# One mask product per attention unit instead of two, and wider sums of h, in a fused attention and SwiGLU kernel

## The chip, the cores and the metric

The kernel runs on one core of a Trainium2 chip. The metric is device time in microseconds (us) of one execution. Four runs of the kernel before are at hand, with their median, and one further execution was taken with the hardware profiler.

## What is computed

The reference is sliding-window attention with a linear distance bias, followed by a SwiGLU feed-forward block. All inputs and the output are float32; the kernel works in float16 with float32 accumulation.

```python
# q, k, v: (8, 8, 576, 64)
scores = (1.0 / np.sqrt(D)) * np.matmul(q, k.transpose(0, 1, 3, 2))
rel = pos[:, None] - pos[None, :]
bias = slopes[:, None, None] * (-np.abs(rel))[None]
mask = (rel >= 0) & (rel < 128)
scores = np.where(mask, scores + bias[None], -1000000000.0)
attn = softmax(scores)                         # max, exp, division by the sum
x = np.matmul(attn, v)                         # then to (4608 tokens, 512)
# w_gate, w_val: (512, 1536), w_out: (1536, 512)
g = x @ w_gate
out = (g * sigmoid(g) * (x @ w_val)) @ w_out
```

## The kernel before

**Attention.** The work is cut into 36 units `i = 9*s + p`: four pairs of sequences `s`, and nine key tiles `p` of 128 rows in each. `scores(i)` writes the score products of all eight heads, 256 queries to a key tile, into four PSUM banks of the pool `ps_a` (tag `a`, four banks in all). ScalarE then takes four exponentials, `act(0,0)`, `act(0,1)`, `act(1,0)`, `act(1,1)` (L284), one for each bank, into the tile `ex` of 128 x 2048 float16 values (eight heads of 256). The mask and the bias are multiplied in afterwards, in place, as exp(bias) from the table `m_reg` (L290, on VectorE): `mul(0)` takes the first four heads after the second exponential, `mul(1)` the other four after the fourth. Units `p` = 3, 7 and 8 have 128 queries and one product at L321 instead, and the units below 4 add the bias in the matmul. `weighted(i)` multiplies with v (PE, L345), VectorE takes the reciprocal of the sums (L347) and scales (L348) into `x`. From unit `LATE` = 13 on, `weighted(i)` is issued in the middle of the scores of unit i+1. `x` is transposed into `xT` on PE (L371) with a copy on ScalarE (L375), or by DMA from SyncE's queue (L366) from unit 24 on.

**Feed-forward.** The tokens form nine blocks `n` of 512. In blocks 0 to 5, for each of the twelve tiles `m` of 128 hidden columns, PE writes `pg` and `pv` (L397; pool `ps_f`, tag `gv`, three banks), ScalarE takes a tanh (L415), VectorE makes `uu` (L416) and `hT` (L427), which free the banks. Block 0 is projected plainly (L451). For blocks 1 to 8 the output product is made by a seven-product scheme (`strassen`, L532). It needs sums of the four quarters of `hT`: per group of tiles four VectorE instructions, L485 to L488, where L486 adds in place into `hT` and L487 and L488 use what L486 and L487 have written. `strassen(n, t)` is spread over the steps of block n+1. Its two accumulators X and Y share one PSUM bank (tile `po`, one buffer), so a product into Y waits until VectorE has read X, and the next product into X until VectorE has read Y. VectorE's additions from X and Y at L536 carry the names `p5s` and `u2s`. Blocks 6 to 8 make gate and value by seven products too (L623), with sums of the weights (L597 to L600) that are made beforehand in block 5 and its neighbours.

**Sums before.** `sums(n, c)` covers two tiles of the lower and two of the upper half of the twelve; it is issued in blocks 1 to 5 at m = 9, 10 and 11 with c = 0, 1, 2, so that each L485 to L488 there handles 128 x 512 values. Except at m = 9 and 10 of block 1, where they are issued at once, the instructions go into the list `later` and leave it one or two at a time at each half step. They come before the third product of the `strassen` of that block. Blocks 6 to 8 issue their sums in another place, in the same groups of two tiles.

**Order.** Generators interleave attention and feed-forward steps. The order on PE is written out from step 60 on, which is near the start of block 2; VectorE, ScalarE and SyncE are ordered by a list scheduler on its own cost estimates at build time, and each engine then runs its queue strictly in that order. VectorE's queue as built is thus fixed before the run: an instruction whose input is not ready holds up all that stand behind it.

Of the kernel before, what the change touches and what calls it, by code (L numbers as in the profile page):

```python
# [36 lines left out]
LATE = 13  # L37
# [14 lines left out]
def kernel(  # L52
# [190 lines left out]
    def scores(i):  # L243

        s, p = units[i]
        def combined(n):
            return scores_128(s, (3, 7, 8)[n], 8, (s, "c", n), msk[n])

        def together(one, two):
            return [one[0] + two[0]] + one[1:] + two[1:]  # L250

        if p == 8:
            first = combined(0) if s == 0 else []
            return first + together(combined(1), combined(2))
        if p == 7 and s == 0:
            return scores_128(s, p, p, (s, p), reg[:, :, 0:P])
        if p == 7:
            return together(scores_128(s, p, p, (s, p), reg[:, :, 0:P]), combined(0))
        if p == 3:
            return scores_128(s, p, p, (s, p), reg[:, :, 0:P], i < FIRST)  # L260
        ks = (9 * s + p) % NK
        banks = []
        early_tile = i < FIRST
        e = epool.tile([P, H, 256], FP16, name="ex", tag="ex", bufs=4)
        ex[(s, p)] = e

        def products():
            for q4 in range(2):
                two = [ps_a.tile([P, 2, 256], FP32, name="ps", tag="a") for _ in range(2)]
                banks.append(two)  # L270
                for par in range(2 if early_tile else 0):
                    o = 4 * q4 + 2 * par
                    nc.tensor.matmul(two[par], idm, bias[:, o:o + 2, :], start=True, stop=False)
                for j in range(2):
                    pair = 2 * q4 + j
                    for par in range(2):
                        rows = slice(64 * par, 64 * par + 64)
                        nc.tensor.matmul(two[par][:, j, :], kT[rows, ks, pair, :],  # L278
                                         qT[rows, p:p + 2, pair, :], start=(j == 0 and not early_tile),
                                         stop=(j == 1))  # L280

        def act(q4, par):
            o = 4 * q4 + 2 * par
            nc.scalar.activation(e[:, o:o + 2, :], banks[q4][par], AF.Exp, scale=scale)  # L284

        def mul(q4):
            if early_tile:
                return
            o = slice(4 * q4, 4 * q4 + 4)
            nc.vector.tensor_mul(e[:, o, :], e[:, o, :], reg[:, o, :])  # L290

        return [[products], [lambda: act(0, 0)], [lambda: act(0, 1), lambda: mul(0)],
                [lambda: act(1, 0)], [lambda: act(1, 1), lambda: mul(1)]]

    def scores_128(s, kt, qt, key, m, early_tile=False):

        ks = (9 * s + kt) % NK
        banks = []
        e = epool.tile([P, H, P], FP16, name="exc", tag="exc", bufs=5)
        ex[key] = e  # L300

        er4 = e.rearrange("k (a par b) q -> k a par b q", a=2, par=2)

        def products():
            banks.extend(ps_a.tile([P, 4, P], FP32, name="psc", tag="a") for _ in range(2))
            for par in range(2 if early_tile else 0):
                nc.tensor.matmul(banks[par].rearrange("k (a b) q -> k a b q", a=2), idm,
                                 bias.rearrange("k (a par b) q -> k a par b q", a=2, par=2)
                                 [:, :, par, :, 0:P], start=True, stop=False)
            for j in range(4):  # L310
                for par in range(2):
                    rows = slice(64 * par, 64 * par + 64)
                    nc.tensor.matmul(banks[par][:, j, :], kT[rows, ks, j, :], qT[rows, qt, j, :],  # L313
                                     start=(j == 0 and not early_tile), stop=(j == 3))

        def act(par):
            nc.scalar.activation(er4[:, :, par], banks[par].rearrange("k (a b) q -> k a b q", a=2),  # L317
                                 AF.Exp, scale=scale)

        return [[products], [lambda: act(0)],  # L320
                [lambda: act(1), lambda: early_tile or nc.vector.tensor_mul(e, e, m)]]  # L321
# [140 lines left out]
    HM = NMB // 2  # L462
# [28 lines left out]
        for f in fs:  # L491
            f()

    def sums(n, c):

        if n not in hsum:
            hsum[n] = [spool.tile([P, HM, 256], FP16, name=f"S{i}", tag=f"S{i}") for i in (2, 3, 4)]
        lo, hi = slice(2 * c, 2 * c + 2), slice(HM + 2 * c, HM + 2 * c + 2)
        a11, a12 = hT[n][:, lo, 0:256], hT[n][:, hi, 0:256]
        a21, a22 = hT[n][:, lo, 256:512], hT[n][:, hi, 256:512]  # L500
        s2, s3, s4 = (t_[:, lo, :] for t_ in hsum[n])
        return four_sums(a11, a12, a21, a22, s2, s3, s4)
# [106 lines left out]
    later = []  # L609
# [91 lines left out]
    def ffn():  # L701

        for n in range(NBLK):
            if n > 1:
                parts = chain(strassen(n - 1, 0), strassen(n - 1, 1))
            if n == 1:
                for j in range(PRE):
                    for _ in project(0, j, ps_f, "po", 1):
                        yield 1.0
            if n == SEVEN_FROM:  # L710
                break
            for m in range(NMB):
                for half, _ in enumerate(gate_val(n, m)):
                    yield 1.0
                    if n > 1 and 2 * m + half in AT:
                        next(parts)
                        yield 0.75
                    if n > 1:
                        for _ in range(1 + (len(later) > 3)):
                            if later:  # L720
                                later.pop(0)()
                if n == 1:
                    if m in (4, 6, 8, 10):
                        for _ in project(0, m // 2 - 2, ps_f, "po", 1):
                            yield 1.0
                    if m in (4, 6, 8):
                        weight_sums(m // 2 - 2)
                if n > 0 and m >= 9:
                    (at_once if n == 1 and m < 11 else later.extend)(sums(n, m - 9))
                if n + 1 == SEVEN_FROM:  # L730
                    if m == SILU_AT:
                        attention_ends()
                        by_silu.update((n, i) for i in range(m + 1, NMB))
                    if m in (SILU_AT + 1, SILU_AT + 2):
                        later.extend(gate_val_weight_sums(m - SILU_AT - 1))
                    if m == SILU_AT:
                        later.extend(x_sums(n + 1))
            if n > 1:
                assert next(parts, 0) == 0
        ends = [strassen(NBLK - 1, t) for t in range(2)]  # L740
        final = ()
        for n, k, name, which in seven_steps():
            if k == 0 and n > SEVEN_FROM:
                assert next(parts, 0) == 0
                parts = chain(strassen(n - 1, 0), strassen(n - 1, 1))
            if n == SEVEN_FROM and k in (1, 3, 10, 17):
                later.extend(gate_val_weight_sums(2 + (k + 4) // 7))
            yield 0.5
            if k % 3 == 2 and k < 42:
                next(parts)  # L750
                yield 0.75
            if k == 20 and n + 1 < NBLK:
                later.extend(x_sums(n + 1))
            if k == 35:
                later.extend(sums(n, 0))
            if name == "fourth" and which is not None and which[1] > 3:
                if which == (NBLK - 1, 5):
                    at_once(final)
                else:
                    later.extend(sums(which[0], which[1] - 3))  # L760
            if n == NBLK - 1 and k == 40:
                final = sums(n, 2)
                later.append(final.pop(0))
            for _ in range(2 if len(later) > 4 or k >= 39 or k < 7 else 1):
                if later:
                    later.pop(0)()
            if n == NBLK - 1 and k == 41:
                next(ends[0])
                yield 0.75
        assert next(parts, 0) == 0 and not later  # L770

        for t in (1, 0, 1, 0, 0, 0, 1, 0, 0, 1, 1, 1, 1):
            next(ends[t])
            yield 0.75
# [230 lines left out]
```

## Time and profile before

| what | value |
|---|---|
| median of 4 runs | 345.08 us (344.95 to 345.47) |
| profiled execution, device time | 344.82 us |
| span of the profile, first to last instruction | 343.0 us |
| granted TensorE clock | 1.000 |
| PE busy | 329.7 us, 2983 matmuls |
| VectorE (DVE) busy | 277.3 us, 652 instructions |
| ScalarE (ACT) busy | 207.7 us, 412 instructions |
| mask products L290, 128 x 1024 | 42, mean 685 ns |
| sums L485 to L488 of hT, 128 x 512 | 24 on each line, mean 415 ns |

The device time is 1.82 us more than the span. By the first `pg` product of each, block 1 runs from 56.5 to 95.5 us, block 2 to 134.4, block 3 to 172.9, block 4 to 210.1 and block 5 to 245; what follows, to 343 us, is blocks 6 to 8. A row of the list of instructions in time gives the start, the time from the first start to the last end of the merged instructions, the engine, the line, what is written and read, the count, and in brackets the idle time of the engine before it with what ended it. [...]

### The profile page before, as it was taken

The page shows a single profiled execution, that of the slowest core. Times are in us where ns is not written, and L with a number is a line of the kernel's source. Part 1 is how long each engine was busy: PE and PEld are TensorE (multiplying, and loading weights), DVE is VectorE, ACT ScalarE, POOL GpSimd, SP SyncE. Part 2 cuts the span into 40 slices and gives each one's busy share as a digit, 9 for nine tenths or more (in the row PEclk, how much of TensorE's full clock was granted, in tenths as well). Part 3 has the DMA queues.
Part 4 walks back from the last instruction along what each step waited for, and adds up shares of the span by engine and source line. Part 5 has one row for each costly group of instructions (what it writes and reads, how often), then busy time and mean ns, then how long its engine had stood idle before and what let it go on. Part 6 is the DMA issues. An engine that isn't in the chain of part 4 may idle for free.

```text
span 343.0 us, 7778 instructions
## 1 busy us (share of the span) xinstructions
PE 329.7 (96%) x2983; PEld 218.7 (64%) x2983; DVE 277.3 (81%) x652; ACT 207.7 (61%) x412; POOL 109.8 (32%) x136
## 2 busy tenths in 40 slices
PE   7999989999999999999999999999999999999995
PEld 4484445444456565656565655565788878888884
DVE  5578886999798679988899999999855975775683
ACT  3758676565666765756556547563467666776640
POOL 8968672639775176743017000000000000000000
PEclk9999999999999999999999999999999999999999
DMA  9999999999999999999949914021101101011014
GB/s 152 169 180 175 161 173 149 83 131 149 153 174 152 158 179 164 162 167 148 185 111 104 176 32 78 15 69 41 63 2 61 63 0 64 7 57 63 0 70 116
DMA packets 160037, 37.37 MB, mean 109 GB/s; under 512 B 147328, under 2 KB 155648, under 8 KB 160000
## 3 DMA queue, kind: packets, MB, share of 16 engines
q0 software_dynamic: 118336, 18.62, 82.5%
q1 hardware_dynamic: 40976, 17.64, 28.6%
q10 hardware_dynamic: 688, 0.62, 0.6%
q8 instruction: 23, 0.38, 0.5%
q14 instruction: 14, 0.11, 0.1%
HBM read 37.91 MB, written 9.44 MB: 138 GB/s over the span
## 4 chain that ended last, share of the span: by engine, by line
PE 70%; DVE 19%; ACT 6%; issue 3%; DMA 1%; ACTq 0%; DVEq 0%
PE po L532 15%; PE pg L397 13%; PE pv L397 12%; PE gX L623 8%; PE gY L623 4%; PE av L345 4%; DVE uu L416 3%; DVE hT L427 3%; PE ps L278 3%; PE p L532 2%; PE po L451 2%; PE gZ L623 2%; DVE x L348 2%; ACT ex L284 2%; PE px L371 2%
## 5 line engine op out<-in xcount | busy, mean ns | idle before, releaser
L397 PE MATMUL pv<-xT,wv_sb 128*128 128x512 f16 (+2 forms) x320 | 76.5, 358 | 0.6 <-DVE uu L416 0.2
L397 PE MATMUL pg<-xT,wg_sb 128*128 128x512 f16 (+2 forms) x320 | 75.8, 358 | 0.3 <-DVE xT L373 0.2
L415 ACT ACTIVATE tt<-pg 128x512 f16<-128x512 f32 (+2 forms) x70 | 41.3, 590 | 50.4 <-PE pg L397 49.5
L284 ACT ACTIVATE ex<-ps 128x512 f16<-128x512 f32 x96 | 50.0, 604 | 11.4 <-PE ps L278 11.4
L416 DVE SCALAR_TENSOR_TENSOR uu<-tt,pg 128x512 f16<-128x512 f16 (+2 forms) x69 | 45.8, 664 | 10.5 <-ACT tt L415 10.2
L427 DVE TENSOR_TENSOR hT<-uu,pv 128x512 f16<-128x512 f16 (+2 forms) x70 | 46.5, 665 | 3.6 <-PE pv L397 1.6
L185 POOL DMA_DIRECT2D va<-in_v_dram x40 | 34.3, 862 | 39.1 <-PE av L345 30.5
L397 PEld LDWEIGHTS <-wg_sb 128*128 128x128 f16 x320 | 28.2, 98 | 24.4 <-issue 2.6
L397 PEld LDWEIGHTS <-wv_sb 128*128 128x128 f16 x320 | 28.3, 98 | 24.1 <-issue 2.9
L532 PEld LDWEIGHTS <-hT 128*128 128x128 f16 x384 | 36.8, 98 | 10.4 <-issue 1.1
L191 POOL DMA_DIRECT2D kn<-in_k_dram x39 | 33.3, 858 | 19.1 <-DMA kT<-kn 11.6
L191 POOL DMA_DIRECT2D qn<-in_q_dram x39 | 33.4, 863 | 15.2 <-DMA va<-in_v_dram 7.8
L532 PEld LDWEIGHTS <-S 128*128 128x128 f16 x288 | 27.7, 98 | 10.6 <-issue 2.5
L290 DVE TENSOR_TENSOR ex<-ex,m_reg 128x1024 f16<-128x1024 f16 x42 | 28.6, 685 | 3.2 <-ACT ex L284 3.1
L348 DVE TENSOR_TENSOR x<-av,rec 128x256 f16<-128x256 f32 x72 | 28.5, 418 | 0.4
L532 PE MATMUL po<-T,S 128*128 128x256 f16 x192 | 26.5, 273 | 0.5 <-DVE S L487 0.5
L532 PE MATMUL po<-T,hT 128*128 128x256 f16 x192 | 26.1, 273 | 0.0
L317 ACT ACTIVATE exc<-psc 128x512 f16<-128x512 f32 x40 | 21.3, 606 | 4.1 <-PE psc L313 4.1
L675 DVE TENSOR_TENSOR hT<-s,v 128x512 f16<-128x512 f16 x18 | 7.6, 422 | 18.5 <-ACT s L674 18.5
L345 PEld LDWEIGHTS <-ex 128*128 128x128 f16 x384 | 17.4, 97 | 4.6 <-issue 1.3
L345 PE MATMUL av<-va,ex 128*128 128x65 f16 x384 | 19.3, 193 | 0.7 <-ACT ex L284 0.7
L278 PE MATMUL ps<-qT,kT 64*128 64x256 f16 x192 | 16.5, 272 | 0.4 <-DVE qT L223 0.2
(134 smaller groups left out, 535.8 us busy)
## 6 DMA issues: line engine op xcount, KB each, us to landing
out_dram<-osb SPq DMA_DIRECT2D x32, 256.0 KB, 2.6
va<-in_v_dram POOLq DMA_DIRECT2D x32, 128.0 KB, 7.9
qn<-in_q_dram POOLq DMA_DIRECT2D x31, 128.0 KB, 8.1
kn<-in_k_dram POOLq DMA_DIRECT2D x31, 128.0 KB, 8.2
wg_sb<-in_moe_w_gate_dram POOLq DMA_DIRECT2D x6, 256.0 KB, 7.6
wv_sb<-in_moe_w_val_dram POOLq DMA_DIRECT2D x6, 256.0 KB, 8.2
wo_sb<-in_moe_w_out_dram POOLq DMA_DIRECT2D x2, 768.0 KB, 9.2
kn<-in_k_dram POOLq DMA_DIRECT2D x8, 64.0 KB, 7.6
```

The costliest lines, as they stand in the source:

```text
L185: nc.gpsimd.dma_start(va[rank][p0:p1, :, 0:D], src)
L191: nc.gpsimd.dma_start(t_[p0:p1], src)
L284: nc.scalar.activation(e[:, o:o + 2, :], banks[q4][par], AF.Exp, scale=scale)
L290: nc.vector.tensor_mul(e[:, o, :], e[:, o, :], reg[:, o, :])
L345: nc.tensor.matmul(av[:, j, :], w, val, start=(n == 0), stop=(n == len(todo) - 1))
L348: nc.vector.tensor_mul(x[:, 4 * half:4 * half + 4, :], av[:, :, 0:D], rec.broadcast_to([P, 4, D]))
L397: nc.tensor.matmul(ps[:, c0:c1], w[:, kb, ms], xT[n][:, kb, c0:c1], start=(kb == 0 and c0 == 0), stop=(kb == NKB - 1 and c1 == 512), skip_ ...
L415: nc.scalar.activation(tt, pg[:, c0:c1], AF.Tanh, scale=0.5)
L416: nc.vector.scalar_tensor_tensor(out=uu, in0=tt, scalar=one if (n, m) == PIN else 1.0, in1=pg[:, c0:c1], op0=ALU.add, op1=ALU.mult)
L427: nc.vector.tensor_mul(hT[n][:, m, c0:c1], acted[(n, m)][1][:, c0:c1], pv[:, c0:c1])
L532: nc.tensor.matmul(dst, a[:, m, cols], b[:, m, :], start=(start and m == 0), stop=(m == HM - 1), skip_group_check=True)
L623: nc.tensor.matmul(dst[:, i, :], w[:, kb, c0 + i * P:c0 + (i + 1) * P], a[:, kb, :], start=(start and i == 0 and kb == 0), stop=(i == 1 an ...
```

## The change

From unit 13 on, `mul(0)` does nothing and `mul(1)`, after the fourth exponential, multiplies all eight heads in one instruction of 128 x 2048 values. This concerns 15 of the 21 units that have L290 products. In blocks 1 to 5 the sums are issued at m = 10 for four tiles of each half (128 x 1024 values in each instruction) and at m = 11 for the remaining two, instead of three times two tiles at m = 9, 10 and 11. The arithmetic on each value is the same.

```diff
@@ scores(i) @@
         def mul(q4):
-            if early_tile:
+            if early_tile or (q4 == 0 and i >= LATE):
                 return
-            o = slice(4 * q4, 4 * q4 + 4)
+            o = slice(0, 8) if i >= LATE else slice(4 * q4, 4 * q4 + 4)
             nc.vector.tensor_mul(e[:, o, :], e[:, o, :], reg[:, o, :])
@@ sums @@
-    def sums(n, c):
+    def sums(n, c, many=2):
...
-        lo, hi = slice(2 * c, 2 * c + 2), slice(HM + 2 * c, HM + 2 * c + 2)
+        lo, hi = slice(2 * c, 2 * c + many), slice(HM + 2 * c, HM + 2 * c + many)
@@ ffn() @@
-                if n > 0 and m >= 9:
-                    (at_once if n == 1 and m < 11 else later.extend)(sums(n, m - 9))
+                if n > 0 and m >= 10:
+                    (at_once if n == 1 and m < 11 else later.extend)(sums(n, 2 * m - 20, 24 - 2 * m))
```

## The prediction

> **What bounds the kernel now.** I read the page's busy shares first, then who PE waits for, then the instructions in time around each wait.
>
> ```profile
> span 343.0 us, 7778 instructions
> PE 329.7 (96%) x2983; PEld 218.7 (64%) x2983; DVE 277.3 (81%) x652; ACT 207.7 (61%) x412; POOL 109.8 (32%) x136
> PEclk9999999999999999999999999999999999999999
> ```
>
> PE is the bound: busy 96% at the full granted clock, and four 512-wide products follow each other in 0.86 us all through the chain. VectorE (DVE) has the second load. The windows tell where the two meet:
>
> ```profile
> 100.00:130.00 30.00, 29.28 (x288) 18.52 (x286) 23.35 (x53) 19.18 (x39) 15.14 (x20) 1.00 1.93 162
> 165.00:194.00 29.00, 27.54 (x247) 16.73 (x245) 28.86 (x73) 15.72 (x33) 7.61 (x10) 1.00 1.50 135
> ```
>
> The columns are PE, weight loads, DVE, ACT, POOL. From 100 to 130 us DVE is busy 23.35 of 30 us; from 165 to 194 it is full. A saving on DVE can only take away waits of PE, and in the part that the change touches (84 to 243 us) these are all that the profile lists (us in total, times, longest):
>
> ```profile
> PE po L532 <- DVE osb L536: 1.5, 2, 0.8
> PE p L532 <- ACT ex L284: 0.7, 1, 0.7
> PE av L345 <- ACT ex L284: 0.7, 2, 0.5
> PE po L532 <- DVE S L487: 0.5, 1, 0.5
> PE px L371 <- DVE x L348: 0.2, 1, 0.2
> PE psc L313 <- DVE osb L536: 0.2, 1, 0.2
> ```
>
> So 2.4 us of waits belong to DVE and 1.4 us to ACT. More than 2.4 us cannot come from a lighter DVE.
>
> **What one instruction less is worth.** The starts of DVE's neighbours in block 1:
>
> ```profile
> 81.03 0.68 DVE L290 TENSOR_TENSOR ex<-ex,m_reg 128x1024 f16<-128x1024 f16 x1
> 81.63 0.41 DVE L486 TENSOR_TENSOR hT<-hT 128x512 f16<-128x512 f16 x1
> 81.97 0.42 DVE L485 TENSOR_TENSOR S<-hT 128x512 f16<-128x512 f16 x1
> 82.31 0.42 DVE L487 TENSOR_TENSOR S<-hT 128x512 f16<-128x512 f16 x1
> ```
>
> The next start is 0.605 us after the 1024-wide product and 0.336 us after a 512-wide sum (81.63 to 82.31 is two of them). So 512 values more cost 0.269 us, and the part paid once per instruction is 0.067 us. The means of 685 and 415 ns would make it 0.145, but they overlap the next start by 0.08 us, so the starts count. A 2048-wide product, which the trace does not show, then takes 0.605 + 2 x 0.269 = 1.14 us of DVE; bounds are 1.08 (twice the slope of values alone, nothing per instruction) and 1.37 (twice the mean of 685). I take the line through the starts, since it is the same operation on the same tiles. The change removes 15 products and 5 x 4 = 20 sums: 35 x 0.067 = 2.3 us of DVE, 5.1 by the means. In a stretch where DVE idles this is worth nothing.
>
> [...]
>
> **What the merged product costs.** It starts only after the fourth exponential, where the first half started after the second, and nothing behind it can pass. I followed the changed kernel's instruction order, as it is built, through all 15 places. The place that counts is in block 2, DVE first, then ACT, then PE:
>
> ```profile
> 126.50 0.69 DVE L416 SCALAR_TENSOR_TENSOR uu<-tt,pg 128x512 f16<-128x512 f16 x1 [1.68 <-ACT tt L415]
> 127.47 0.69 DVE L290 TENSOR_TENSOR ex<-ex,m_reg 128x1024 f16<-128x1024 f16 x1 [0.29 <-ACT ex L284]
> 128.09 0.68 DVE L427 TENSOR_TENSOR hT<-uu,pv 128x512 f16<-128x512 f16 x1
> 128.68 0.42 DVE L536 SCALAR_TENSOR_TENSOR osb<-po,p5s 128x256 f32<-128x256 f32 x1
> ```
> ```profile
> 126.36 2.06 ACT L284 ACTIVATE ex<-ps 128x512 f16<-128x512 f32 x4
> ```
> ```profile
> 128.10 1.02 PE L397 MATMUL pg<-xT,wg_sb 128*128 128x512 f16 x4
> 129.15 0.81 PE L532 MATMUL po<-wo_sb,S 128*128 128x256 f16 x6
> ```
>
> Before, the `p5s` addition ends at 129.10, and PE, free at 129.12, starts its product into the shared bank at 129.15. DVE had just idled 1.68 us there. After, the order is uu, hT, the whole product, then `p5s` (the second half stood behind it before). hT starts at 127.37, as its product ends at 127.34. The whole product starts when the exponentials end, 126.36 + 2.06 = 128.42, plus 0.03; the addition starts 1.14 us later, at 129.59, and ends at 130.01. PE's product starts at 130.05: **+0.90 us**, between 0.84 and 1.13 by the bounds of the product. Queued behind on DVE are reciprocals, x and uu, which PE needs 2 us later; on PE everything is behind.
>
> Elsewhere the cover holds or nearly. The product delays what follows it by up to 0.53 us where its first half used to run during the third and fourth exponential. Behind it `p5s` at 148.82 has 0.53 us until PE needs it (**+0.05** for the edge), x at 181.09 is 0.24 us early and moves by 0.29 (**+0.05**), `p5s` at 205.09 has 0.38 and moves by 0.30, `uu`, `hT` and x elsewhere have 0.4 us and more. If a cover is gone, each costs what it lacks, at most 0.3 us.
>
> **Block 1.** Here the scheduler also reorders PE between 87.4 and 93 us. On DVE x at 85.25 comes 0.33 us earlier, and px with it, but the next product waits for an exponential that ends at 86.27, as before: 0. Then in the new order four of the po products, not five, stand ahead of the av products, and the second pair of ps waits for its bank until 88.77 (first exponential from 88.17). That gives the first av at 89.36 for 89.79, and the second at 89.82 for 90.04, as its exponential ends at 89.76. From there PE runs seven po (1.51), eight pg and pv (1.72), px and av (0.45) without a wait, to the ps at 93.50 for 93.86. The x copy on ACT now stands behind the tanh, ends at 93.80 and frees the bank of the last four ps. The exponentials start at 93.91 for 94.28, and av follows at 94.56 for 94.93: **-0.37 us**. It is between 0 (the queue slips back behind one of these waits) and -0.6 (all the ACT wait of 0.46, and one change of product kind, 0.1). The whole product there ends 0.2 us before PE needs the x behind it; if not, +0.3 at most.
>
> **Where DVE is full.** From 130 to 143 us the removed instructions and the later PE put DVE 0.57 us ahead, which ends PE's wait for x at 142.9: ps starts there at 143.01 and 143.33, 0.10 and 0.19 late, of which I take **-0.25**. From 164.7 to 188.2 DVE never idles; six instructions less (four sums, two products) give 0.40 us, but the new order pulls one more weight sum (L599, 0.34, right behind the one that it needs) ahead of `p5s`, so the wait of 0.84 us at 187.8 stays: 0. From 205 to 217.5 the sums and products give 0.40, but the product at 201.6 now starts with the fourth exponential (201.97) and ends 0.31 later: **-0.06** on the 0.5 us wait for S at 217.4. The wait of 0.62 at 167.2 begins with an ACT wait, not with load: 0. Transposes and stores on SyncE's queue keep their count; in block 1 three transposes move ahead of a store, whose data come later anyway. POOL's order is the same. The ACT wait of 0.7 at 118 stands behind a tanh, not behind DVE, and after 243 nothing is changed: 0.
>
> **The sum.** -0.37 + 0.90 + 0.05 + 0.05 - 0.25 - 0.06 = +0.32 us on the profiled 344.82 (343.0 span and 1.82 around it), so 345.1. The median of the runs is 345.08, 0.26 above that execution, and on it I predict **345.4 us**. With the ends of the terms the case spans -0.5 to +1.6: 344.6 to 346.7. A measurement of this kernel tells about 0.2%, 0.7 us, from no change, so most of the case lies within that.
>
> [...]
>
> **Rivals.** *Relief reaches PE.* In the full stretches the 0.40 us saved shows at 187.8 and again at 217.4, with -0.37 and -0.25 of above, and the whole product does not stand in PE's way: -1.4, so 343.7. For it speaks that 1.5 us of the waits lie there; against it the order as built, with the product ahead of `p5s` and L599 pulled forward. 18%. *The merged product holds PE up at more places.* If it takes 1.23 us and not 1.14 (twice the mean of 685 less one time the 0.145 that the means give per instruction), the wait in block 2 is 0.99 and the thin covers give way: 0.14 at 149, 0.14 at 181, 0.01 at 205; with block 1 at 0 and the -0.25 kept that is +1.0: 346.1. It decides from some 0.1 us of extra length on; against it speaks that the starts of the 512- and 1024-wide rows leave no room for it. 30%. *The change does not do what it says*, in that the scheduler splits or duplicates work: excluded, as the built order has 15 products of 2048 and 617 DVE instructions for 652. The forecast has 52%.
>
> **Numbers.** 0.2% of the median puts the bounds at 344.4 and 345.8. The first rival's 343.7 lies below, the second's 346.1 above, and a sixth of the forecast's own case (-0.5 to +1.6, likeliest +0.3) lies above too. Faster by over 0.2%: 0.18; within: 0.46; slower: 0.36. The range 344.0 to 346.5 leaves out some half of the first rival and the ends of the others.
>
> **What would show it.** Right: L290 at 128 x 2048 spaced 1.14 us to the next start; a PE wait for L536 of 0.9 us near 129 to 130 us that was 0.03; the waits at 167 and 188 still there; av in block 1 0.4 us earlier. Wrong: no new wait there, or the L536 wait at 188 gone, or new waits for x, uu or hT of over 0.3 us behind the products.

## The result, and the profile after

The changed kernel takes 345.52 us (median of 35 runs) where the kernel before, run beside it, takes 345.00 (55 runs): a ratio of 1.0014, with a 95% interval from 1.0009 to 1.0019, or +0.3 to +0.7 us. The prediction was 345.4 us, in a range of 344.0 to 346.5. By the 0.2% of the prediction this is no change; the interval shows a slight loss.

Page and list of groups of the changed kernel (out<-in, shapes, count | busy us, mean ns | idle time of the engine before it):

```profile
span 344.4 us, 7743 instructions
PE 329.7 (96%) x2983; PEld 219.1 (64%) x2983; DVE 275.6 (80%) x617; ACT 207.6 (60%) x412; POOL 109.6 (32%) x136
```
```profile
L290 DVE TENSOR_TENSOR ex<-ex,m_reg 128x2048 f16<-128x2048 f16 x15 | 18.3, 1221 | 4.3 <-ACT ex L284 4.2
L290 DVE TENSOR_TENSOR ex<-ex,m_reg 128x1024 f16<-128x1024 f16 x12 | 8.1, 687 | 0.9 <-ACT ex L284 0.8
```

PE is as busy as before, DVE has 35 instructions less. In front of its mask products DVE now idles 5.2 us, waiting for exponentials, where that was 3.2 us in all.

The windows (PE, weight loads, DVE, ACT, POOL) of the two stretches shown of before:

```profile
100.00:130.00 30.00, 28.81 (x282) 18.03 (x281) 22.95 (x46) 19.42 (x39) 15.18 (x19) 1.00 2.03 159
...
165.00:194.00 29.00, 27.64 (x258) 16.73 (x256) 28.40 (x64) 16.31 (x34) 7.59 (x10) 1.00 1.44 138
```

DVE is lighter in both (22.95 for 23.35 us, 28.40 for 28.86). From 100 to 130 us, where it had room, PE has lost 0.47 us of busy time, to a wait that begins at 129.50 and that the window's end cuts in two; from 165 to 194, where it was full, PE has 0.10 more. The windows stand at fixed times, and the changed kernel runs 0.4 to 1.4 us late in them, so these figures are only rough; the table below compares place by place.

The waits of PE from 84 to 243 us in the changed kernel:

```profile
PE po L532 <- DVE osb L536: 2.3, 3, 0.9
PE p L532 <- ACT ex L284: 0.7, 1, 0.7
PE av L345 <- ACT ex L284: 0.6, 2, 0.4
PE po L532 <- DVE S L487: 0.4, 1, 0.4
PE psc L313 <- DVE osb L536: 0.2, 1, 0.2
```

One wait for the L536 additions is new, two were there before; the wait of px for x is gone. The new one is in block 2. DVE, PE and ACT there, from the list of instructions in time of the changed kernel:

```profile
127.76 0.69 DVE L427 TENSOR_TENSOR hT<-uu,pv 128x512 f16<-128x512 f16 x1 [0.20 <-PE pv L397]
128.84 1.23 DVE L290 TENSOR_TENSOR ex<-ex,m_reg 128x2048 f16<-128x2048 f16 x1 [0.39 <-ACT ex L284]
129.98 0.42 DVE L536 SCALAR_TENSOR_TENSOR osb<-po,p5s 128x256 f32<-128x256 f32 x1
```
```profile
128.48 1.02 PE L397 MATMUL pg<-xT,wg_sb 128*128 128x512 f16 x4
130.45 0.81 PE L532 MATMUL po<-wo_sb,S 128*128 128x256 f16 x6 [0.95 <-DVE osb L536]
```
```profile
126.74 2.06 ACT L284 ACTIVATE ex<-ps 128x512 f16<-128x512 f32 x4
```

The exponentials end at 128.80, the whole product starts at 128.84, the addition 1.14 us behind it, and PE stands idle for 0.95 us. Before, the addition had gone ahead.

The times of the two profiled executions, 346.16 and 344.82 us, are not a fair pair: in the one of the changed kernel the first load of q landed later, and everything from there on is 0.65 us late. PE in the changed kernel, then in the kernel before:

```profile
6.57 0.66 PE L211 MATMUL pt<-stage 128*128 128x128 f32 x4 [0.48 <-DMA stage<-in_q_dram]
```
```profile
5.91 0.66 PE L211 MATMUL pt<-stage 128*128 128x128 f32 x4
```

Taking that off, the start of the same matmul in both kernels gives what each place adds to the time of PE (us; the last two columns are experiments 3 and 4, each against before in the same way):

| place, us in before | predicted | changed kernel | products alone | sums alone |
|---|---|---|---|---|
| block 1, to 93 | -0.37 | -0.27 | +0.07 | -0.27 |
| 129, `p5s` in block 2 | +0.90 | +0.92 | +0.91 | 0 |
| 143, ps | -0.25 | -0.10 | -0.10 | -0.10 |
| 149, `p5s` in block 3 | +0.05 | +0.13 | +0.13 | 0 |
| 181, ps behind x | +0.05 | +0.06 | +0.44 | 0 |
| 188, `p5s` in block 4 | 0 | -0.11 | -0.23 | -0.37 |
| 217 to 219, S and `p1s` | -0.06 | -0.13 | +0.16 | -0.29 |
| sum | +0.32 | +0.50 | +1.4 | -1.0 |

The sum of the trace, +0.50, agrees with the ratio of the medians (+0.48). The rest of the 1.34 us between the two profiled executions, 0.2, lies behind PE's last product.

### The profile page after: what moved, and what is told of

Read it like the earlier page. It is cut to its first block, busy times and chain, and to the rows that moved or that the text cites. A ratio compares the mean times of both kernels' runs of the same rounds, so it can differ in the third digit from the quotient of the medians.

```text
span 344.4 us, 7743 instructions
## 1 busy us (share of the span) xinstructions
PE 329.7 (96%) x2983; PEld 219.1 (64%) x2983; DVE 275.6 (80%) x617; ACT 207.6 (60%) x412; POOL 109.6 (32%) x136
## 4 chain that ended last, share of the span: by engine, by line
PE 75%; DVE 14%; ACT 6%; issue 3%; DMA 2%; SPq 0%; DVEq 0%; ACTq 0%
PE po L532 15%; PE pg L397 14%; PE pv L397 14%; PE gX L623 8%; PE gY L623 4%; PE av L345 4%; PE po L451 3%; PE ps L278 3%; PE p L532 3%; DVE uu L416 3%; ACT ex L284 3%; PE gZ L623 2%; DVE hT L427 2%; DMA stage<-in_q_dram 2%; PE px L371 1%
## 5 line engine op out<-in xcount | busy, mean ns | idle before, releaser
L290 DVE TENSOR_TENSOR ex<-ex,m_reg 128x2048 f16<-128x2048 f16 (+1 forms) x27 | 26.5, 984 | 5.1 <-ACT ex L284 5.0
L375 ACT COPY xT<-px 128x512 f16<-128x512 f16 x20 | 11.7, 584 | 9.1 <-PE px L371 8.9
```

## The experiments

In the kernels of experiments 1, 2 and 6 to 10 an added line moves the numbers behind it by one: L536 becomes L537, L487 L488, L599 L600. In experiment 5 they move by three.

**1. One whole product, at 129 us.**

```diff
-            if early_tile:
+            whole = i in (19,)
+            if early_tile or (q4 == 0 and whole):
                 return
-            o = slice(4 * q4, 4 * q4 + 4)
+            o = slice(0, 8) if whole else slice(4 * q4, 4 * q4 + 4)
```

> The kernel before with one edit: unit 19's mask product, the one near 128 us, is whole; all other products and all sums stay as before. PE, ACT and POOL keep their order. Theory A (the whole product waits for the fourth exponential and stands ahead of the p5s addition in DVE's order): a PE wait for L536 of 0.9 us near 129 to 130 us, and +0.6 to +0.9 us in all, since DVE gains up to 0.25 us on a later PE behind it: 345.6 to 345.9. Theory B (the added time comes from the many merged products together, or from the new order in block 1): within 0.2 us of before. Theory C (a lighter DVE pays): no slower than before.

Measured: 345.74 us for 345.07 of before beside it, ratio 1.0021 (1.0013 to 1.0030). The list of this kernel shows the place:

```profile
128.46 1.23 DVE L291 TENSOR_TENSOR ex<-ex,m_reg 128x2048 f16<-128x2048 f16 x1 [0.38 <-ACT ex L284]
129.60 0.42 DVE L537 SCALAR_TENSOR_TENSOR osb<-po,p5s 128x256 f32<-128x256 f32 x1
...
130.07 0.81 PE L533 MATMUL po<-wo_sb,S 128*128 128x256 f16 x6 [0.95 <-DVE osb L537]
```

PE is 0.92 us late from here, 0.82 from 143 us on. One merged product makes a loss larger than that of the whole change. B and C fall for this place.

**2. The changed kernel with that product in halves.**

```diff
-            if early_tile or (q4 == 0 and i >= LATE):
+            whole = i >= LATE and i not in (19,)
+            if early_tile or (q4 == 0 and whole):
```

> The changed kernel with unit 19's product in two halves again; the other fourteen are whole and the sums stay in fours. PE, ACT and POOL keep the order of the changed kernel. Theory A: the wait near 129 us is gone (under 0.1 us), the time is 0.7 to 0.9 us below the changed kernel, 344.6 to 344.8, and so 0.2 to 0.5 below the kernel before. Theory B: 0 to 0.2 us below the changed kernel, 345.3 to 345.5. Theory C: as A at this place, since it is silent on the rest.

Measured: 344.54 us for 345.07 of before, ratio 0.9984 (0.9975 to 0.9993), and 0.98 below the changed kernel's 345.52 (0.88 by the trace). DVE, then PE, in this kernel:

```profile
128.78 0.42 DVE L537 SCALAR_TENSOR_TENSOR osb<-po,p5s 128x256 f32<-128x256 f32 x1
```
```profile
129.25 0.82 PE L533 MATMUL po<-wo_sb,S 128*128 128x256 f16 x6
```

PE follows without a wait. A holds; the change with 14 merged products is a small gain.

**3. The products alone** (`sums` as before).

> The kernel before with the mask products alone changed (15 whole products, the sums in pairs). Theory A: the wait of 0.9 us near 129 us as in the changed kernel, the edge near 149 us (+0.1), and less of the gains in block 1 and near 143 us, which need the sums' order and their saved instructions: +0.7 to +1.1 us, 345.7 to 346.1. Theory B: +1.0 or more with several new waits of 0.1 us or more elsewhere. Theory C: faster than before.

Measured: 346.40 us for 345.07, ratio 1.0050 (1.0031 to 1.0069), more than A's +0.7 to +1.1. The table says where: +0.91 at 129 us is as large as in the changed kernel, but 181 us costs 0.44, where the changed kernel loses 0.06, and 217 us costs 0.16. At 188 us PE then waits less for `p5s`, and 0.23 comes back. DVE at 178 to 183 us, then the weight loads that go with PE's score products (PEld), in this kernel:

```profile
178.52 0.41 DVE L599 TENSOR_TENSOR kT<-wv_sb,kT 128x512 f16<-128x512 f16 x1
178.85 0.42 DVE L487 TENSOR_TENSOR S<-hT 128x512 f16<-128x512 f16 x1
179.19 0.42 DVE L600 TENSOR_TENSOR kT<-wg_sb,kT 128x512 f16<-128x512 f16 x1
179.53 1.22 DVE L290 TENSOR_TENSOR ex<-ex,m_reg 128x2048 f16<-128x2048 f16 x1
...
182.71 0.41 DVE L348 TENSOR_TENSOR x<-av,rec 128x256 f16<-128x256 f32 x1
```
```profile
183.18 0.11 PEld L278 LDWEIGHTS <-kT 64*128 64x128 f16 x3 [0.44 <-DVE x L348]
```

In the kernel before, the two weight sums L599 and L600 come behind this x (at 182.35 and 183.29, x at 181.09); here they stand ahead of unit 27's whole product. So x is 1.62 us later than before while PE is 1.01 late: 0.61, two sums of 0.34 less one saved instruction of 0.07. The changed kernel pulls only L599 ahead here. A has the places at 129 and 149 us right, but not the sum. Over 1.0 us with further losses of 0.13, 0.44 and 0.16 us is what B named, so B holds for the products alone.

**4. The sums alone** (each product in halves).

> The kernel before with the sums alone changed (groups of four and two, every product in halves). It has the new order of PE and ACT in block 1. Theory A: no new wait near 129 us; block 1 gives 0.27 us as in the changed kernel, the wait for x near 143 us up to 0.1: -0.3 to -0.5 us, 344.5 to 344.7. Theory B, if block 1's new order costs time: +0.2 or more. If block 1's gain needs the whole product there: within 0.1 us of before.

Measured: 344.15 us for 345.07, ratio 0.9980 (0.9966 to 0.9994), by the trace -1.02. That is more than A expected, from two places that A did not name, 188 and 217 us. Block 1's gain is the sums' alone.

**5. One instruction more.** Instead of nothing, the place of unit 19's first half gets an operation that only takes time.

```diff
         def mul(q4):
+            if q4 == 0 and i == 19:
+                nc.vector.tensor_tensor(e[:, 0:4, :], e[:, 0:4, :], e[:, 0:4, :], op=ALU.max)
+                return
             if early_tile or (q4 == 0 and i >= LATE):
```

> The changed kernel with one instruction more: in unit 19, where the first half of the product used to stand, VectorE takes the maximum of the first four heads of ex with themselves, in place (128 x 1024, the values stay as they are). The whole product stays whole. As built, this instruction comes behind uu, and the p5s addition now stands ahead of the whole product; PE, ACT and POOL keep the order of the changed kernel. Theory A (what costs is the place in the queue, a wait for the fourth exponential ahead of p5s): the wait near 129 us goes, and with 0.6 us more of VectorE work the time falls by 0.6 to 0.9 us, to 344.6 to 344.9. Theory B (the length of the merged product, or VectorE's load, costs): 0 to 0.6 us slower than the changed kernel, 345.5 to 346.1.

Measured: 344.83 us for 344.96 of before, ratio 0.9994 (0.9985 to 1.0003), 0.69 below the changed kernel's median. DVE, then PE, in this kernel's list:

```profile
127.46 0.69 DVE L288 TENSOR_TENSOR ex<-ex 128x1024 f16<-128x1024 f16 x1 [0.29 <-ACT ex L284]
128.07 0.68 DVE L430 TENSOR_TENSOR hT<-uu,pv 128x512 f16<-128x512 f16 x1
128.67 0.41 DVE L539 SCALAR_TENSOR_TENSOR osb<-po,p5s 128x256 f32<-128x256 f32 x1
...
129.88 1.22 DVE L293 TENSOR_TENSOR ex<-ex,m_reg 128x2048 f16<-128x2048 f16 x1
```
```profile
129.13 0.81 PE L535 MATMUL po<-wo_sb,S 128*128 128x256 f16 x6
```

The product is as long as in the changed kernel and DVE has 0.6 us more to do, yet PE's wait is gone, since the addition is now ahead of the product. So neither length nor load cost the 0.92 us; the place in the queue did. The added load shows further on: at 143 us PE loses 0.17 us here, where it gains 0.10 in all the other kernels here.

**6. The sums and unit 28's product, at 184 us.** (As in 1, with `i in (28,)`, on the changed sums.)

> The kernel with the sums alone changed (344.15 us) and one whole product more, that of unit 28, near 184 us. As built, one more weight sum (L599) then stands ahead of that product and of the p5s addition for which PE waits at 188 us; PE and ACT keep their order. Theory A (the gain of 0.37 us that the sums alone bring at 188 us is undone in the changed kernel by L599, 0.34 us, less 0.07 for the instruction saved): +0.2 to +0.3 us at 188 us, 344.35 to 344.45. Theory B (the whole product itself holds PE up there): +0.4 or more. Theory C (one instruction less is a gain): -0.07 at 188 us, 344.1.

Measured: 344.50 us for 344.96, ratio 0.9983 (0.9974 to 0.9991). DVE ahead of `p5s`, and PE's wait, in this kernel:

```profile
183.56 0.41 DVE L598 TENSOR_TENSOR qT<-wv_sb,wg_sb 128x512 f16<-128x512 f16 x1
184.01 0.43 DVE L600 TENSOR_TENSOR qT<-wv_sb,qT 128x512 f16<-128x512 f16 x1
184.35 1.22 DVE L291 TENSOR_TENSOR ex<-ex,m_reg 128x2048 f16<-128x2048 f16 x1
...
188.62 0.81 PE L533 MATMUL po<-wo_sb,S 128*128 128x256 f16 x6 [0.84 <-DVE osb L537]
```

The same wait in the kernel with the sums alone, and in the changed kernel:

```profile
188.31 0.82 PE L532 MATMUL po<-wo_sb,S 128*128 128x256 f16 x6 [0.48 <-DVE osb L536]
```
```profile
189.92 0.81 PE L532 MATMUL po<-wo_sb,S 128*128 128x256 f16 x6 [0.73 <-DVE osb L536]
```

From the kernel with the sums alone to this one the wait grows from 0.48 to 0.84 us, with the order of PE unchanged; the changed kernel has 0.73. The pulled weight sum starts 0.45 behind its neighbour (184.01 - 183.56) and not 0.34; it reads what that one has just written. Less 0.07 for the saved instruction, that is 0.38, and by the trace PE loses 0.38 between the two kernels. DVE has no idle time ahead of the product, so B, the product's own wait, is not what costs. A holds with a price 0.1 higher, and the median lies 0.05 above A's range; C falls.

**7. The sums and unit 33's product, at 215 us.** (As in 6, with `i in (33,)`.)

> The kernel with the sums alone changed and one whole product more, that of unit 33, near 215 us. As built, the product, uu, two reciprocals and two x then stand ahead of the sum L487 into S for which PE waits at 217 us; with halves, that sum comes early and the second half behind it. Theory A (the whole product brings the wait for S back): a wait for L487 of 0.3 to 0.5 us where the sums alone have none, +0.1 to +0.3 us there, 344.25 to 344.45. Theory C (one instruction less is a gain): 344.1.

Measured: 343.87 us for 344.96, ratio 0.9966 (0.9954 to 0.9979). Theory A falls here. The waits of PE from 215 to 219 us in this kernel, and in the one with the sums alone:

```profile
PE po L533 <- DVE S L488: 0.2, 1, 0.2
PE psc L314 <- DVE osb L537: 0.2, 1, 0.2
```
```profile
PE psc L313 <- DVE osb L536: 0.5, 1, 0.5
```

The wait for S is back, but the wait for the `p1s` addition behind it (L537 here, from the tile `p`) is shorter by more: with halves, the second one stood ahead of that addition. The two orders share out one and the same debt of DVE, and PE is 0.05 us earlier here by the trace, 0.07 in all, about one saved instruction (0.067). That is C.

**8. Eleven whole products** (19, 28, 32 and 33 in halves).

> The changed kernel with the products of units 19, 28, 32 and 33 in two halves; the other eleven whole, the sums in fours and twos. Theory A: no new wait at 129 us, the waits at 188 and 217 us as with the sums alone, so 344.0 to 344.3, 1.2 to 1.5 us below the changed kernel and 0.7 to 1.0 below the kernel before. Theory B (many whole products cost together): 344.6 or more.

Measured: 344.25 us for 344.96, ratio 0.9978 (0.9969 to 0.9986), in A's range. By the trace the parts are not all A's: 188 us gives 0.50 us and not 0.37, but 217 us gives 0.01 and not 0.29, as unit 31's whole product is still there (experiment 9). At 149 us PE is 0.13 us late, as in the changed kernel: unit 22's whole product is still there.

**9. The sums with units 31 and 33 whole.** (As in 7, with `i in (31, 33)`.)

> The kernel with the sums changed and unit 33 whole (343.87 us), and unit 31's product, near 202 us, whole as well. PE, ACT and POOL keep their order. Theory A (that product then waits on VectorE, idle, for the fourth exponential, and what stands behind it is 0.2 to 0.3 us later up to the waits at 217 and 218 us): an idle time of VectorE of about 0.2 us ahead of it, and +0.2 to +0.3 us at 217 to 218 us, 344.05 to 344.2. Theory C (one instruction less is a gain): 343.8.

Measured: 344.15 us for 345.13, ratio 0.9971 (0.9960 to 0.9982). DVE at 201 us and PE at 217 in this kernel, then both in the kernel of experiment 7:

```profile
201.39 1.23 DVE L291 TENSOR_TENSOR ex<-ex,m_reg 128x2048 f16<-128x2048 f16 x1 [0.22 <-ACT ex L284]
202.53 0.25 DVE L348 RECIPROCAL rec<-av 128x4 f32<-128x4 f32 x2
...
217.30 0.39 PE L533 MATMUL po<-T,S 128*128 128x256 f16 x2 [0.47 <-DVE S L488]
```
```profile
201.61 0.68 DVE L291 TENSOR_TENSOR ex<-ex,m_reg 128x1024 f16<-128x1024 f16 x1
202.21 0.24 DVE L348 RECIPROCAL rec<-av 128x4 f32<-128x4 f32 x2
...
217.00 0.39 PE L533 MATMUL po<-T,S 128*128 128x256 f16 x2 [0.17 <-DVE S L488]
```

The idle 0.22 us and the rest of the product put DVE 0.32 us behind at 202 us, and 15 us later PE is 0.30 late. DVE does not catch up in between: its uu at 215 us is still 0.30 behind (215.35 for 215.05). A holds.

**10. Ten whole products** (19, 22, 27, 28 and 31 in halves).

> The changed kernel with the products of units 19, 22, 27, 28 and 31 in two halves, the five behind which an addition or a sum for PE stood thin; the other ten whole, the sums in fours and twos. Theory A: no new wait at 129, 149 and 181 us, the gains of the sums alone at 188 us and of unit 33's whole product at 217 us: 343.6 to 343.9. Theory B (many whole products cost together): 344.2 or more.

Measured: 344.08 us for 345.13, ratio 0.9968 (0.9956 to 0.9979), a little above A's range. PE shows no step at 149 and 181 us any more. It and experiment 7, with one whole product, are the fastest kernels here, and their intervals can't be told apart: nine more merged products bring nothing that shows. The gain is the sums', about 1 us or 0.3% below before, where the whole change lost 0.5.

## Why the prediction was right

- **The main term.** Predicted +0.90 us at 129 us by hT, whole product, `p5s` in this order; measured +0.92. Each step shows: the product starts 0.04 us behind the exponentials and takes 1.14 us to the next start, as the line through the 512- and 1024-wide starts said. Experiments 1, 2 and 5 pin it to the place in the queue.
- **Block 1**, -0.37, measured -0.27. The av products came at the times worked out (89.79 us for 89.82, the late load taken off). What was mis-sized stands between them and the next ps: the sum had four pv in 0.86 us, but ps starts 0.96 behind the first pv. It does so in the kernel before too, so the 0.10 could have been read there. The changed kernel, then the kernel before:

```profile
93.28 1.03 PE L397 MATMUL pv<-xT,wv_sb 128*128 128x512 f16 x4
94.24 0.63 PE L278 MATMUL ps<-qT,kT 64*128 64x256 f16 x8
```
```profile
92.90 1.03 PE L397 MATMUL pv<-xT,wv_sb 128*128 128x512 f16 x4
93.86 0.61 PE L278 MATMUL ps<-qT,kT 64*128 64x256 f16 x8
```

- **143 us**, -0.25, measured -0.10. The same step failed: of the two delays of ps I had put down both to x. And the 0.19 of the second counts the 0.10 of the first again, so that no more than 0.19 was there. In experiment 2, where the second pair follows the first without a wait, the first still starts 0.96 behind pv (142.15 to 143.11). So 0.10 us is the change from pv to ps and was never to be had; only the rest, 0.09 to 0.10, went. This wait for x stands with the weight load in the kernel before:

```profile
143.32 0.11 PEld L278 LDWEIGHTS <-kT 64*128 64x128 f16 x4 [0.20 <-DVE x L348]
```

The list of PE's waits, from which the prediction drew its 2.4 us, therefore lacks it, as that of experiment 3 lacks the 0.44 us at 181.

- **149 us**, +0.05, measured +0.13; **181 us**, +0.05, measured +0.06. The edges were there, and one was thinner than I sized it.
- **188 us**, 0, measured -0.11. The saved instructions pay (-0.37 with the sums alone), and the pulled weight sum takes that back (0.38, experiment 6), though its step was sized at 0.34 and is 0.45. What is left fits unit 27's saved instruction (0.07) and the 0.06 lost at 181 us, which a full DVE need not add again; no run separates these two.
- **217 us**, -0.06, measured -0.13: the later product of unit 31 costs 0.31, as predicted (0.30 in experiment 9), and what the saved instructions give is a little more than 0.4. The prediction's own parts, 0.40 less 0.31, make -0.09 and not -0.06.
- **The rivals.** *Relief reaches PE* is what the sums alone do, at both places it named; it lost since two merged products (28 and 31) take it back and a third adds 0.92. Its 343.7 us is near the 343.87 of experiment 7. *The merged product holds PE up at more places* had the right edge at 149 us (0.13 for 0.14), but the product is 1.14 us long and block 1's gain stayed. Without the sums, in experiment 3, PE is held up at 181 us too, not by a longer product but by the two weight sums pulled ahead of it.

The total is right within 0.2 us partly by chance: the gains of -0.37 and -0.25 were too large by 0.25 and 149 us cost 0.08 more, while the gains at 188 and 217 us were too small by 0.18.

The sums alone gained 0.66 us at 188 and 217 us, where DVE was full or nearly so (28.86 of the 29 us from 165 to 194 and 23.98 of the 25 to 219 in the kernel before); unit 19's product lost 0.92 in block 2, where DVE had room (23.35 of the 30 us from 100 to 130 before).

## What to carry to other kernels

Merging two instructions of VectorE's queue saved 0.07 us here (two halves at 0.605 us from start to start against 1.14 for the whole product), but the merged one waited for its last input, and all that stood behind it waited too, which cost PE 0.92 us at 129 us: look up who waits for the next few instructions before counting the saving. Merge those whose inputs are all ready (the sums), and leave in halves those that follow a producer piece by piece and stand ahead of something that the bound engine needs. After such an edit read the order as built, since a scheduler also moves instructions that the edit doesn't touch (L599 in experiment 6, 0.38 us; L599 and L600 in experiment 3, most of the 0.44 us).

## What the runs showed of the hardware

- Between four 512-wide products on PE and the score products of 64 rows there are 0.96 us from start to start, and 0.86 to the next group of their own kind: 0.10 us for the change of kind, at 23 of 24 such places in the kernel before and as many in the changed one, and without a wait of PE for another engine in the profile (the 24th has 1.11 us, 0.08 of them a wait). What takes the 0.10 us is not shown.
- A 512-wide operation on DVE that reads what the one right ahead has written starts 0.45 us after it, where independent ones follow in 0.34 (L599 behind L597, 184.85 to 185.30 us in the changed kernel). L487 right behind L486 and L488 right behind L487, 512-wide, follow in 0.45 to 0.46 too, at eight places in the kernel before and seven in the changed one; 1024-wide they follow in 0.72 (two places in the changed kernel), where most other 1024-wide ones take 0.60 to 0.61 to the next start.
- The first load of q landed later in the profiled execution of the changed kernel than in that of the kernel before (PE starts behind it at 6.57 us for 5.91), and all that follows is moved by 0.65 us, more than the effect that was to be measured (0.48 by the medians); the profile of experiment 1 is not moved (uu at 126.50 us there and in the kernel before). Here only the start of the same matmul in both traces, with that shift taken off, shows which part is the change.
